# First small sums by copying and adding DMA, and one convolution tap moved to the second layer, in a two-layer kernel

## Chip, core and metric

The kernel runs on one core of a Trainium2 chip. The metric is the device time of one execution in microseconds, of three runs: 2356.79, 2358.98 and 2359.99, so a median of 2358.98 us.

## What is computed

A depthwise causal convolution over seven tokens with softmax weights for each of 8 heads, then a two-layer feed-forward with a hard-swish between, all in float32. `x` is 8 x 4096 x 192; the feed-forward is 192 to 2048 to 192 over 32768 tokens.

```python
w = softmax(weight, axis=-1)                  # 8 heads x 7 taps
out[b, s, h, g] = sum_k w[h, k] * x_pad[b, s + k, h, g]
h = out.reshape(32768, 192) @ w_in            # 192 -> 2048
g = h * np.clip(h + 3.0, 0.0, 6.0) / 6.0
y = g @ w_out                                 # 2048 -> 192
```

## The kernel before, in words

The tokens go in 32 blocks of 1024 (`TB`). The first block (block 0) is computed together with the preparation of the weights; blocks 1 to 31 run through the same two functions, `first_layer` and `second_layer`, which write out the whole order of the instructions by hand (the scheduler is in manual mode; it only adds the waits). Every engine executes its own instructions in the order in which the program gives them.

**First layer** (L499 to L562). Sixteen slots n; each computes 128 columns of the hidden layer for the 1024 tokens. A slot has 18 matmuls in three parts, HIGH, LOW and MIX (a float32 product made of three faster ones, L506). `begin(n)` issues HIGH and LOW and lets ScalarE scale the two banks (L523); for the last slot ScalarE scales the lower bank (L526) and VectorE the upper one (L527). `end(n)` issues MIX, ScalarE's relu (L302) and VectorE's gate (L306). The program runs `begin` two slots ahead of `end`. Slots 0 to 7 read the block's own tokens (`y_own`), slots 8 to 15 read the same tokens with the partition halves swapped (`y_other`, swapped by DMA, L265 to L267). Slots 0 to 7 fill the quarters A11 and A22 of the hidden activations `g`, slots 8 to 15 A21 and A12. Each quarter is 128 partitions by 8 chunks by 512 tokens. Between the slots stand jobs: `jobs` holds the convolution taps of the next block (L1033, one VectorE instruction each), and after them come small sums for the second layer.

**Second layer** (L604 to L891). The product with `w_out` is done by a Strassen-like scheme (Winograd's form, seven products): S1 = A21 + A22, S2 = S1 - A11, S3 = A11 - A21, S4 = A12 - S2, and the products n = 1 to 7 of `prod` (L417). S1, S2 and S4 are formed in place over A21, A11 and S3. S1 is formed by adding DMAs (`third_sum`, L564): GpSimd issues a transfer with `accum_op=add` of a pair of chunks, 512 KB, once the same pair of S3 has been taken from A21. Products 1, 2, 4 and 5 are cut once more in the same way for a part of the output (`small`, L657): their small sums s1 to s4 of the four parts of a quarter (`small_sums`, L575) lie in `shared` (of A11), `sums4[0]` (of A22), `sums2` (of A12) and `s5` (of S1, over A22). The fourth small sum of A22 and of A12 (`last_sum`, L703) and S4 (`negative`, L700) are formed by `difference` (L696): ScalarE writes the negative of one operand, then a DMA issued by GpSimd adds the other.

TensorE works here in four columns of 32 (streams 0 to 3). `put` gives each matmul a place on a clock of 80 units, one unit being 256 tokens; `do(t, fn)` puts other engines' work between the matmuls at t - 0.5. L885 sorts all of it by clock, and so fixes the order in which each engine gets its instructions. `plain(j, bank, n, q, chunks)` puts product n's matmuls over chunks into stream j, `level_two` (L727) puts the small products in an order and, behind each, a copy on ScalarE that hands the partial sum to the next accumulator (`steps`). `fill` puts pieces of product 5 into gaps of stream 3.

`between` (L1099 to L1107) holds the work for later blocks: splitting the next block's `y` into HIGH, LOW and MIX (L1050 to L1060), swapping them, loading x of the block after (`begin_conv`, on SP's queue) and that block's first convolution product on ScalarE (L1031). The tile `x` has one buffer, so a load waits for the last tap that reads it. `shared` also holds the outputs of the block before, which are stored from there.

Stores and x loads are issued by SP, the swaps and all adding DMAs by GpSimd. All run on the core's 16 DMA engines.

Of the kernel before, what the change touches and what calls it, by code (L numbers as in the profile page):

```python
# [8 lines left out]
ALU = mybir.AluOpType  # L9
# [16 lines left out]
def kernel(  # L26
# [472 lines left out]
    def first_layer(i, jobs):  # L499
# [44 lines left out]
        for n in range(count):  # L544
            if n == count - 3:
                begin(n + 2)
            end(n)
            if n < count - 3:
                begin(n + 2)
            for job in jobs.get(n, ()):  # L550
                job()
            if n < NP and n % 2:
                small_sums(shared, A11, (1, 2, 3, 4), nc.gpsimd, every[n - 1 : n + 1])
            if n == NP:
                sums4[:] = [pools[0].tile([P, NP, N], F32, name="z4", tag="own")]
                small_sums(sums4[0], A22, (1,), nc.gpsimd)
            if n == count - 3:
                small_sums(sums4[0], A22, (2,), nc.vector)
            if n in (NP + 1, NP + 3, NP + 5):
                third_sum((n - NP - 1) // 2, nc.gpsimd if n < NP + 5 else nc.vector)  # L560
            if n == NP + 1:
                small_sums(sums4[0], A22, (3,), nc.gpsimd)  # L562

    def third_sum(p, engine):  # L564
        pair = slice(2 * p, 2 * p + 2)
        g_sums(engine, (3,), range(NP)[pair], 2)
        nc.gpsimd.dma_start(out=S1[:, pair], in_=A22[:, pair], accum_op=ALU.add)  # L567
# [7 lines left out]
    def small_sums(to, x, which, engine=nc.gpsimd, r=every):  # L575

        r = slice(r[0], r[-1] + 1)
        x11, x12, x21, x22 = four_parts(x[:, r])
        s1, s2, s3, s4 = four_parts(to[:, r])
        forms = {  # L580
            1: (s1, x21, x22, ALU.add), 2: (s2, s1, x11, ALU.subtract),
            3: (s3, x11, x21, ALU.subtract), 4: (s4, x12, s2, ALU.subtract),
        }
        for n in which:
            o, p, q, op = forms[n]
            engine.tensor_tensor(out=o, in0=p, in1=q, op=op)  # L586
# [17 lines left out]
    def second_layer(i, between):  # L604
# [91 lines left out]
        def difference(out, x, y):  # L696
            nc.scalar.mul(out, y, -1.0)  # L697
            nc.gpsimd.dma_start(out=out, in_=x, accum_op=ALU.add)  # L698

# [47 lines left out]
        def fill(k):  # L747
            plain(3, b, 5, 2, [chunks.pop(0) for _ in range(k)], first_fill.pop() if first_fill else False)
# [41 lines left out]
        level_two(5, lambda: late["p5"], (1,))  # L790
        plain(3, a, 2, 2, every[2:6])
        last or fill(2)
# [21 lines left out]
        do(0, small_sums, sums2, A12, (1, 2), nc.vector)  # L814
        do(5, last_sum, sums4[0], A22)
        do(6, third_sum, 3, nc.vector)
        do(7, small_sums, sums2, A12, (3,), nc.vector)
# [3 lines left out]
        do(33, g_sums, nc.vector, (2,), every[4:], 4)  # L821
# [3 lines left out]
        do(36, small_sums, s5, S1, (1, 2, 3, 4), nc.vector)  # L825
# [87 lines left out]
    with tc.manual_schedule():  # L913
# [144 lines left out]
        def split_mix():  # L1058
            high, low, mix = y_own
            from_high(mix[:], high[:], 1.0 + EPS, y[:], ALU.subtract)  # L1060
# [30 lines left out]
        for i in range(1, NB):  # L1091
            jobs = {n: [tap] for n, tap in zip((-1, 1, 3, 5, 8, 11), taps)}
# [7 lines left out]
            if i + 1 < NB:  # L1100
                between += [(37, split_high), (56, split_low), (63, split_mix)]
                between += [
                    (t, lambda n=n: swap_parts(nc.gpsimd, (n,)))
                    for n, t in ((HIGH, 70), (LOW, 70), (MIX, 70))
                ]
            if i + 2 < NB:
                between += [(1, begin_conv), (74, lambda: conv[0]())]  # L1107
            left = second_layer(i, between)
            taps = conv[1:]
# [33 lines left out]
```

## Time and profile before

| What | Value |
|---|---|
| runs | 2356.79, 2358.98, 2359.99 us |
| the profiled execution: time, span | 2358.78, 2357.0 us |
| mean granted TensorE clock | 0.997 |
| blocks 1 to 31 start at | 99.75 us; block 31 at 2273.8 us |
| a middle block (13), from 969.45 us | 72.45 us: first layer 35.34, second 37.11 |
| first layer's matmuls in a block | 288, 128x512, 0.113 us apart |
| second layer's | 80 units of 0.43 us |
| ScalarE's scaling L523, relu L302 | 1.01, 1.11 us |
| VectorE's gate L306, tap L1033 | 1.21, 2.25 us (mean) |
| adding DMAs, per block | 4 of g, 4 of s, 2 of z, 512 KB each |
| DMA traffic | 296.94 MB, 126 GB/s in the mean |

The profile is one execution, taken by the hardware profiler. Its page gives for each engine its busy time, the share of the span and the number of instructions, then the groups of instructions by line and shape, with how long the engine idled before them and what released it. PE is TensorE's matmuls, PEld its weight loads, DVE is VectorE, ACT ScalarE, POOL GpSimd, SP SyncE. L636 is line 636 of the kernel. Names such as `z<-g` are the tile written and the tile read: `z` is the tile of the small sums of A22 and of A12, `s` is S3, `shared` the small sums of A11 and the outputs. A float32 matmul of the second layer stands in the trace as two instructions. The waits list says who waited for whom, the total, how many times and the longest; the timeline gives start, duration, engine, line, operation, and in brackets the idle time before it with what ended it.

### The profile page before, as it was taken

To read this page: it belongs to the slowest core of one execution; us is meant where nothing else is said; L and a number is where in the kernel's file an instruction comes from. 1 tells how busy PE (TensorE), PEld (TensorE's weight loads), DVE (VectorE), ACT (ScalarE), POOL (GpSimd) and SP (SyncE) were. 2 spreads that over 40 slices of the span, in tenths; PEclk is the share of its full clock that TensorE was granted. 3 is DMA by queue.
4 is the path that set the end of the run, shared out by engine and by line. 5 is a ranking of instruction groups with operands and counts; after the bars stand their busy time and mean duration, and the time that the engine had idled before them with its cause. 6 is when DMAs were issued, how large, how long until landed. Compare 5 with 4: busy or idle time off the path is not lost.

```text
span 2357.0 us, 55204 instructions
## 1 busy us (share of the span) xinstructions
PE 2276.9 (97%) x22984; PEld 1508.2 (64%) x22984; DVE 2027.7 (86%) x1859; ACT 1762.2 (75%) x2391; POOL 1338.0 (57%) x1157
## 2 busy tenths in 40 slices
PE   9999999999999999999999999999999999999998
PEld 5456666566666566666676656666666766666664
DVE  8888988888888898888888888888889888888876
ACT  7578787777777787777878777777778777777875
POOL 2456664466654666545666446665466654566644
PEclk9999999999999999999999999999999999999999
DMA  5376668866678666687666886667866668766576
GB/s 148 68 128 120 123 112 148 145 116 122 117 132 157 112 122 123 116 157 132 119 123 114 144 150 113 120 119 129 157 115 123 123 113 158 135 118 123 107 135 104
DMA packets 336939, 296.94 MB, mean 126 GB/s; under 512 B 211984, under 2 KB 248848, under 8 KB 336688
## 3 DMA queue, kind: packets, MB, share of 16 engines
q0 software_dynamic: 114976, 234.46, 55.8%
q1 hardware_dynamic: 220472, 58.67, 13.9%
q8 instruction: 181, 2.97, 0.5%
q14 instruction: 70, 0.57, 0.1%
q10 hardware_dynamic: 1240, 0.27, 0.1%
HBM read 31.72 MB, written 25.17 MB: 24 GB/s over the span
## 4 chain that ended last, share of the span: by engine, by line
PE 55%; ACT 12%; DMA 12%; DVE 11%; issue 9%; POOL 1%; DVEq 0%; SPq 0%; ACTq 0%; POOLq 0%
PE psum L636 30%; PE psum L511 22%; DMA z<-g 11%; ACT g L302 6%; DVE g L306 5%; ACT psum L523 3%; DVE y L1033 3%; PE psum L296 2%; PE psum L341 2%; ACT psum L633 1%; DVE s L414 1%; DVE psum L527 1%; POOL g L567 1%; ACT z L735 0%; ACT shared L735 0%
## 5 line engine op out<-in xcount | busy, mean ns | idle before, releaser
L636 PE MATMUL psum<-g,w_out 128*32 128x512 f32 (+1 forms) x5968 | 893.4, 506 | 3.9 <-DMA g<-g 3.9
L636 PE MATMUL psum<-s,w_out 128*32 128x512 f32 (+1 forms) x3024 | 692.3, 587 | 1.5 <-DMA s<-g 1.5
L306 DVE SCALAR_TENSOR_TENSOR g<-g,psum 128x1024 f32<-128x1024 f32 (+1 forms) x528 | 613.0, 1181 | 75.6 <-ACT g L302 75.2
L302 ACT ACTIVATE g<-psum,half 128x1024 f32<-128x1024 f32 (+1 forms) x528 | 568.1, 1087 | 38.1 <-PE psum L511 37.3
L511 PE MATMUL psum<-y_other,w_in 64*128 64x512 f32 x4464 | 542.4, 391 | 42.8 <-DVE psum L527 41.4
L511 PE MATMUL psum<-y_own,w_in 64*128 64x512 f32 x4464 | 523.8, 390 | 0.0
L511 PEld LDWEIGHTS psum<-y_other,w_in 64*128 64x128 f32 x4464 | 418.4, 184 | 156.1 <-DVE psum L527 53.6
L523 ACT ACTIVATE psum<-psum 128x1024 f32<-128x1024 f32 x465 | 468.7, 1008 | 62.1 <-PE psum L511 56.6
L636 PEld LDWEIGHTS psum<-g,w_out 128*32 128x32 f32 x5968 | 361.3, 110 | 219.5 <-issue 105.1
L586 POOL TENSOR_TENSOR shared<-g 128x256 f32<-128x256 f32 x248 | 365.3, 1473 | 237.6 <-DVE g L306 237.6
L511 PEld LDWEIGHTS psum<-y_own,w_in 64*128 64x128 f32 x4464 | 422.6, 184 | 108.9 <-issue 26.0
L1033 DVE SCALAR_TENSOR_TENSOR y<-x,c_sb,y 128x1536 f32<-128x1536 f32 x186 | 418.6, 2251 | 1.5 <-ACT y L1031 1.3
L698 POOL DMA_DIRECT2D s<-g x124 | 148.4, 1197 | 266.6 <-ACT s L697 266.6
L636 PE MATMUL psum<-g,w_s 128*32 128x256 f32 x1488 | 283.0, 380 | 0.0
L636 PE MATMUL psum<-z,w_out 128*32 128x256 f32 x992 | 235.9, 381 | 23.7 <-DMA z<-g 21.2
L636 PE MATMUL psum<-z,w_s 128*32 128x256 f32 x992 | 236.7, 382 | 0.2 <-DVE z L586 0.2
L567 POOL DMA_DIRECT2D g<-g x124 | 149.5, 1206 | 152.5 <-DVE s L414 130.3
L636 PEld LDWEIGHTS psum<-s,w_out 128*32 128x32 f32 x3024 | 181.9, 110 | 70.7 <-issue 32.9
L636 PEld LDWEIGHTS psum<-z,w_out 128*32 128x32 f32 x992 | 103.7, 110 | 125.3 <-DMA z<-g 47.6
L266 POOL DMA_DIRECT2D y_other<-y_own x90 | 47.9, 532 | 236.0 <-DVE shared L458 235.9
L414 DVE TENSOR_TENSOR g<-g 128x2048 f32<-128x2048 f32 x62 | 142.1, 2293 | 32.8 <-issue 31.7
L586 POOL TENSOR_TENSOR z<-g 128x1024 f32<-128x1024 f32 x62 | 163.2, 2632 | 0.0
(114 smaller groups left out, 2932.8 us busy)
## 6 DMA issues: line engine op xcount, KB each, us to landing
y_other<-y_own POOLq DMA_DIRECT2D x180, 384.0 KB, 8.0
g<-g POOLq DMA_DIRECT2D x124, 512.0 KB, 6.5
s<-g POOLq DMA_DIRECT2D x124, 512.0 KB, 6.4
z<-g POOLq DMA_DIRECT2D x62, 512.0 KB, 8.3
out_dram<-shared SPq DMA_DIRECT2D x378, 64.0 KB, 4.3
x<-in_x_dram SPq DMA_DIRECT2D x53, 388.5 KB, 7.7
stage<-in_moe_w_in_dram SPq DMA_DIRECT2D x16, 192.0 KB, 4.4
stage<-in_moe_w_out_dram SPq DMA_DIRECT2D x8, 384.0 KB, 5.6
```

Of the source, the lines that this page charges most:

```text
L266: dma.dma_start(out=to[D2:P], in_=part[0:D2])
L296: nc.tensor.matmul(out=psum[:, b], lhsT=w[r], rhs=src, start=start, stop=stop, skip_group_check=onto,)
L302: nc.scalar.activation(r6, h, ACT.Relu, bias=half[:], scale=1.0 / 6.0)
L306: nc.vector.scalar_tensor_tensor(out=g_, in0=g_, scalar=1.0, in1=h, op0=ALU.min, op1=ALU.mult)
L414: engine.tensor_tensor(out=o[:, r], in0=a[:, r], in1=b[:, r], op=op)
L511: nc.tensor.matmul(out=psum[:, 2 * slots[n] + k], lhsT=r32(w_in_parts[part][r, c, s]), rhs=r32(y_other[0][r, part, s] if group else y_own[ ...
L523: nc.scalar.mul(both(n), both(n), 4097.0)
L567: nc.gpsimd.dma_start(out=S1[:, pair], in_=A22[:, pair], accum_op=ALU.add)
L586: engine.tensor_tensor(out=o, in0=p, in1=q, op=op)
L636: nc.tensor.matmul(out=out, lhsT=w, rhs=x, start=start, stop=True, tile_position=(0, j * QS), skip_group_check=True,)
L698: nc.gpsimd.dma_start(out=out, in_=x, accum_op=ALU.add)
L1033: jobs.append(lambda k=k: nc.vector.scalar_tensor_tensor(out=y[:], in0=x[:, :, k : k + N], scalar=c_sb[:, k : k + 1], in1=y[:], op0=ALU.mu ...
```

## The change

In the first layer the sum s1 = x21 + x22 of A11 and of A22 is no longer computed by GpSimd. Once slots 0 to 7 are done, SP issues for each a DMA that copies x21 to s1, and one slot later GpSimd issues for each a DMA that adds x22. The second small sum, until now s1 - x11, is written as x22 - s3, which is the same since s3 = x11 - x21, so that it follows the third. The third sum of A22 is formed by `difference` at slot 8: ScalarE writes -x21, an adding DMA adds x11. A22's second sum moves from VectorE at slot 13 to GpSimd at slot 11.

S3's pairs 0 and 1 stay on GpSimd at slots 9 and 11; pair 2 moves from VectorE at slot 13 to VectorE at the second layer's start; pair 3 is formed by `difference` (ScalarE and an adding DMA) in place of VectorE. The adding DMAs of S1's pairs 2 and 3 are issued in the second layer behind A22's fourth sum and S3's last pair.

In the second layer the first small product of product 5 moves from clock 36 to 44 (not in the last block), and four plain matmuls of product 2 move ahead of it. The small sums of S1 on VectorE are done third and second first, ahead of the second half of S2, then first and fourth. The second convolution product of the block after next (a tap on VectorE) moves from the first layer into the second, at 62, and the first one on ScalarE from 74 to 58. MIX is computed from LOW and HIGH in place of `y` and HIGH, at 70; the swaps stand at 69, 69 and 71.

```diff
--- before.py
+++ after.py
@@ -550,21 +550,37 @@
             for job in jobs.get(n, ()):
                 job()
             if n < NP and n % 2:
-                small_sums(shared, A11, (1, 2, 3, 4), nc.gpsimd, every[n - 1 : n + 1])
+                small_sums(shared, A11, (3, 2, 4), nc.gpsimd, every[n - 1 : n + 1])
             if n == NP:
                 sums4[:] = [pools[0].tile([P, NP, N], F32, name="z4", tag="own")]
-                small_sums(sums4[0], A22, (1,), nc.gpsimd)
-            if n == count - 3:
-                small_sums(sums4[0], A22, (2,), nc.vector)
-            if n in (NP + 1, NP + 3, NP + 5):
-                third_sum((n - NP - 1) // 2, nc.gpsimd if n < NP + 5 else nc.vector)
+                for to, x in ((shared, A11), (sums4[0], A22)):
+                    nc.sync.dma_start(out=four_parts(to)[0], in_=four_parts(x)[2])
+                difference(four_parts(sums4[0])[2], four_parts(A22)[0], four_parts(A22)[2])
             if n == NP + 1:
-                small_sums(sums4[0], A22, (3,), nc.gpsimd)
-
-    def third_sum(p, engine):
-        pair = slice(2 * p, 2 * p + 2)
-        g_sums(engine, (3,), range(NP)[pair], 2)
-        nc.gpsimd.dma_start(out=S1[:, pair], in_=A22[:, pair], accum_op=ALU.add)
+                third_sum(0)
+                add_pair(0)
+                for to, x in ((shared, A11), (sums4[0], A22)):
+                    adding(four_parts(to)[0], four_parts(x)[3])
+            if n == NP + 3:
+                small_sums(sums4[0], A22, (2,), nc.gpsimd)
+                third_sum(1)
+                add_pair(1)
+
+    def adding(out, x):
+        nc.gpsimd.dma_start(out=out, in_=x, accum_op=ALU.add)
+
+    def difference(out, x, y):
+        nc.scalar.mul(out, y, -1.0)
+        adding(out, x)
+
+    def pair_of(p):
+        return slice(2 * p, 2 * p + 2)
+
+    def third_sum(p, engine=nc.gpsimd):
+        g_sums(engine, (3,), every[pair_of(p)], 2)
+
+    def add_pair(p):
+        adding(S1[:, pair_of(p)], A22[:, pair_of(p)])
 
     TH = N // 2
     halves = slice(0, TH), slice(TH, N)
@@ -578,7 +594,7 @@
         x11, x12, x21, x22 = four_parts(x[:, r])
         s1, s2, s3, s4 = four_parts(to[:, r])
         forms = {
-            1: (s1, x21, x22, ALU.add), 2: (s2, s1, x11, ALU.subtract),
+            1: (s1, x21, x22, ALU.add), 2: (s2, x22, s3, ALU.subtract),
             3: (s3, x11, x21, ALU.subtract), 4: (s4, x12, s2, ALU.subtract),
         }
         for n in which:
@@ -693,10 +709,6 @@
             add(p[second, hi], p[second, hi], p[second, lo])
             add(p[second, lo], m136, p[second, lo])
 
-        def difference(out, x, y):
-            nc.scalar.mul(out, y, -1.0)
-            nc.gpsimd.dma_start(out=out, in_=x, accum_op=ALU.add)
-
         def negative(pair):
             difference(S3[:, pair], A12[:, pair], S2[:, pair])
 
@@ -787,9 +799,11 @@
         fill_half(0, 4) if last else fill(2)
         level_two(1, lambda: p1, rest)
         fill_half(0, 4) if last else fill(2)
-        level_two(5, lambda: late["p5"], (1,))
+        last and level_two(5, lambda: late["p5"], (1,))
         plain(3, a, 2, 2, every[2:6])
-        last or fill(2)
+        if not last:
+            level_two(5, lambda: late["p5"], (1,))
+            fill(2)
         level_two(5, lambda: late["p5"], rest)
         fill_half(1, 8) if last else fill(2)
         assert clock == [80] * 4
@@ -811,18 +825,21 @@
         def fold_with(p, j=3):
             fold(p, chains[j][2])
 
-        do(0, small_sums, sums2, A12, (1, 2), nc.vector)
-        do(5, last_sum, sums4[0], A22)
-        do(6, third_sum, 3, nc.vector)
-        do(7, small_sums, sums2, A12, (3,), nc.vector)
+        do(4.5, last_sum, sums4[0], A22)
+        do(1, third_sum, 2, nc.vector)
+        do(6, lambda: difference(S3[:, pair_of(3)], A11[:, pair_of(3)], A21[:, pair_of(3)]))
+        do(6, add_pair, 2)
+        do(6, add_pair, 3)
+        do(7, small_sums, sums2, A12, (3, 2, 1), nc.vector)
         do(28.5, g_sums, nc.vector, (2,), every[:4], 4)
         do(32, tiles)
         do(32, fold_with, p1)
-        do(33, g_sums, nc.vector, (2,), every[4:], 4)
+        do(35, small_sums, s5, S1, (3, 2), nc.vector)
+        do(35.5, g_sums, nc.vector, (2,), every[4:], 4)
         do(32.5, fold_with, p4, 2)
         do(36, copy, out=b[m], in_=p1)
         do(21, last_sum, sums2, A12)
-        do(36, small_sums, s5, S1, (1, 2, 3, 4), nc.vector)
+        do(36, small_sums, s5, S1, (1, 4), nc.vector)
         for n, t in zip(range(0, NP, 2), (34, 39, 42, 45)):
             do(t, negative, slice(n, n + 2))
         do(45.5, lambda: copy(out=late["p7"], in_=c[m]))
@@ -1057,7 +1074,7 @@
 
         def split_mix():
             high, low, mix = y_own
-            from_high(mix[:], high[:], 1.0 + EPS, y[:], ALU.subtract)
+            from_high(mix[:], high[:], EPS, low[:], ALU.subtract)
 
         def prepare():
             for n in range(0, NP, 4):
@@ -1089,7 +1106,7 @@
         left = []
         taps = conv[2:]
         for i in range(1, NB):
-            jobs = {n: [tap] for n, tap in zip((-1, 1, 3, 5, 8, 11), taps)}
+            jobs = {n: [tap] for n, tap in zip((-1, 1, 3, 5, 8), taps)}
             jobs[-1] = left + jobs.get(-1, [])
             first_layer(i, jobs)
             def begin_conv():
@@ -1098,15 +1115,15 @@
 
             between, conv = [], []
             if i + 1 < NB:
-                between += [(37, split_high), (56, split_low), (63, split_mix)]
+                between += [(37, split_high), (57, split_low), (70, split_mix)]
                 between += [
                     (t, lambda n=n: swap_parts(nc.gpsimd, (n,)))
-                    for n, t in ((HIGH, 70), (LOW, 70), (MIX, 70))
+                    for n, t in ((HIGH, 69), (LOW, 69), (MIX, 71))
                 ]
             if i + 2 < NB:
-                between += [(1, begin_conv), (74, lambda: conv[0]())]
+                between += [(1, begin_conv), (58, lambda: conv[0]()), (62, lambda: conv[1]())]
             left = second_layer(i, between)
-            taps = conv[1:]
+            taps = conv[2:]
 
 
 # ---- launch: one core; inputs and outputs as the reference has them ----
```

## Prediction

> **What bounds the kernel now.** I read first the page's busy times, then the whole list of waits, then one middle block (969.45 to 1041.90 us, 72.45 us long) in stretches, then its queues in order of time.
>
> ```profile
> PE 2276.9 (97%) x22984; PEld 1508.2 (64%) x22984; DVE 2027.7 (86%) x1859; ACT 1762.2 (75%) x2391; POOL 1338.0 (57%) x1157
> ```
>
> The waits give the total in us, how many, and the longest:
>
> ```profile
> PE psum L511 <- DVE psum L527: 41.4, 29, 1.5
> PE psum L636 <- DMA z<-g: 21.2, 29, 1.4
> ```
>
> TensorE is the bound, and it stands still in two places of each block: at the end of the first layer, where the last scaling waits on VectorE, and in the second layer, where the fourth sum of A22 has not landed. Per block that is 1.4 and 0.7 us by PE's rows; matmul starts, which show the pace, lose about 1.7 us at each.
>
> The first place, VectorE in order of time:
>
> ```profile
> 998.71 3.38 DVE L1033 SCALAR_TENSOR_TENSOR y<-x,c_sb,y 128x1536 f32<-128x1536 f32 x1
> 1002.02 1.21 DVE L306 SCALAR_TENSOR_TENSOR g<-g,psum 128x1024 f32<-128x1024 f32 x1
> 1003.15 0.69 DVE L527 TENSOR_SCALAR psum<-psum 128x512 f32<-128x512 f32 x1
> ```
>
> The convolution tap of slot 11 took 3.38 us (1.78 where GpSimd is quiet), and the scaling L527 stands behind it.
>
> The second place needs the DMA engines. The stretches below have PE, PEld, DVE, ACT, POOL busy, then PEclk, the DMA engines' share, GB/s:
>
> ```profile
> 969.45:982.45 13.00, 13.00 (x117) 10.99 (x116) 11.36 (x11) 11.49 (x12) 5.20 (x7) 1.00 0.99 207
> 982.45:992.45 10.00, 9.96 (x88) 7.83 (x86) 9.69 (x8) 9.52 (x11) 9.77 (x11) 1.00 0.01 2
> 992.45:1001.45 9.00, 9.00 (x84) 7.44 (x82) 8.18 (x5) 8.60 (x9) 8.70 (x6) 1.00 0.01 2
> 1005.95:1009.45 3.50, 3.50 (x44) 2.08 (x40) 3.50 (x3) 1.81 (x4) 2.18 (x3) 1.00 1.04 236
> 1009.45:1024.45 15.00, 14.21 (x181) 8.45 (x177) 11.74 (x12) 9.20 (x21) 5.17 (x5) 1.00 1.09 176
> 1024.45:1038.45 14.00, 14.00 (x174) 7.48 (x170) 11.96 (x14) 10.26 (x17) 4.38 (x4) 1.00 0.96 161
> ```
>
> The DMA engines idle for 19 us of the first layer and are full through the second. GpSimd issues the adding DMAs one after another:
>
> ```profile
> 1009.27 1.20 POOL L567 DMA_DIRECT2D g<-g  x1 [1.01 <-DVE s L414]
> 1010.93 1.28 POOL L698 DMA_DIRECT2D z<-g  x1 [0.46 <-ACT psum L732]
> 1015.20 1.18 POOL L567 DMA_DIRECT2D g<-g  x1 [2.98 <-DVE s L414]
> 1016.94 1.28 POOL L698 DMA_DIRECT2D z<-g  x1 [0.57 <-PE psum L636]
> ```
>
> By the trace's landings these four and the pair before them (issued at 1007.04) landed at 43.5, 46.1, 49.6, 52.2 and 55.1 us from the block's start: in order, 2.6 us apart for a pair sum (2 KB packets) and 3.5 and 2.9 us for a fourth sum (1 KB packets). So a full queue serves a pair in 2.6 and a strided sum in 3.2 us. The S3 negations behind them landed 3.1, 3.1 and 3.3 us apart.
>
> **The change, part by part.** Times are from the block's start.
>
> *Tap and sums off VectorE in the first layer.* The slot 11 tap (3.38), A22's second sum (2.96 beside GpSimd) and the third pair's S3 (1.21) leave VectorE before the end of the layer. Against this ScalarE gets one multiplication at slot 8 (1.06, as L697) in a queue without slack: L523 and L302 start 0.92 and 1.12 us apart, 2.04 per slot, and PE's 18 matmuls at 0.113 take 2.04. The lag stays to the end of the layer, but each scaling is needed only 1.03 us after it ends, and 0.35 us of idle is there at slot 10. I charge 0.3. The last block's first layer, without the wait, took 33.0 us, the typical one 35.34; I take 33.3, bounds 33.0 and 34.4. In itself this is worth 2.0 us.
>
> *GpSimd* loses four ops of 0.74 and two 128x1024 sums (2.4 each) and gains one such sum and four issues of 1.2. It is not the bound; it only sets when DMAs start.
>
> *Six more transfers of 512 KB per block*: two copies on SP's queue, two adds onto them, A22's third, S3's last pair. The trace has no plain 1 KB copy inside SBUF. Bounds: 403 GB/s, the best slice while the x loads ran, gives 1.3 us; the slower adding row gives 3.5. I take 2.5, between the 2.2 of the x loads' mean (236 GB/s) and the 3.0 of 176 GB/s.
>
> When does this work start? The copies need the gate of slot 7, which ends at 21.3; a store's first packet comes 1.4 us after its issue, so 22.7. The x tile is free after the tap of slot 8 (24.5) and no longer after that of slot 11 (32.6), so both x loads (3.4 us, the 1005.95 stretch) move up into the same stretch. GpSimd's issues: A22's third at 25.4 (behind its sums of A11 and the multiplication), pair 0 at 29.0, the two adds at 30.7 and 32.4, then A22's second sum and S3's second pair (2.4 each), pair 1 at 38.3, the fourth sum at 39.9, S3's last pair at 41.6, pairs 2 and 3 at 43.2 and 44.9 (spaced 1.66, as 1009.27 to 1010.93). Each starts moving 1.8 us after its issue (pair 0 issued at 31.33 has its first packet at 33.13), or when those ahead are done, and here those ahead are later every time. So the landing of pair 3, L, is a plain sum:
>
> 22.7 + copies 5.0 + A22's third 3.2 + x 3.4 + pair 0 2.6 + adds 6.4 + pair 1 2.6 + fourth sum 3.2 + S3's last pair 3.1 + pairs 2 and 3 5.2 + 0.3 to signal = 57.7.
>
> Before, L was 52.2.
>
> *New waits on GpSimd.* Its two adds wait for the copies (landed by 30), and A22's second sum, now x22 minus the third, waits for the third's landing: 31.2 if the x loads queue behind it, 34.6 if ahead. In the second case GpSimd stands 1.4 us, with S3's second pair, pair 1, the fourth sum and all later issues behind it; L does not move, since each of these is still issued before its turn in the line (pair 1 would be ready at 41.5, its turn is 43.3).
>
> *What hangs on pair 3.* The small sums of S1 are reordered: third and second now stand ahead of the second half of S2 on VectorE. From L: 1.14 + 1.24 for these, 2.22 for S2's half. Only then can ScalarE negate pairs 2 and 3, and the moved step of product 5 (copy of its first small product, clock 47.5 instead of 39.5) is now queued behind them: 1.06, two copies 0.73, 1.06, 0.59, the copy 0.36; with waits 8.5 us from L. The matmuls of clock 52 need that copy, and 28 units of 0.43 follow: 12.0. So a block lasts L + 20.5 = 78.2 us, 5.75 more than now. The first layer's 2.0 us are not in this sum: TensorE arrives sooner and waits longer (at units 28 and 32 for the fourth sum and S3's last pair, 49.4 and 52.5, then at 44 and 52).
>
> *The rest, at nothing.* S3's third pair (1.21) moves to the second layer's start on VectorE and S3's last pair leaves it for ScalarE (1.06, where ScalarE idles 1.6 us before L732); both are done before the transfers they feed have their turn. A12's small sums only change order; unit 24 needs them at 43.7, they end near 41. The second-layer tap (1.69) takes split_mix's old place (1.71) on VectorE; split_mix at 69.5 only delays the swap, whose last landing (10.8 us into the next block) has until the switch to the swapped parts at 19.8; without that cover each us costs one. The wait before unit 36 is for a ScalarE copy (L633) that stays. Small product (5,1) at clock 44 costs nothing by itself.
>
> **Sum.** 29 blocks at +5.75 are 167; block 30 loads no x: 5.75 - 3.4 = 2.4; in the last block the step keeps its old place, and unit 36 waits for L = 54.3 instead of running at about 51: 3.3. The profiled execution took 2358.8 us (span 2357.0, median of the runs 2359.0): 2358.8 + 172 = 2531.
>
> The ends: copies at 1.3 and each adding transfer 0.15 faster give L near 54 and +2 per block, about 2420; copies at 3.5, pairs at 2.95 (16 packets of 185 ns on each engine) and strided adds at 3.5 (32 of 110 ns) give L near 62 and +10, about 2660.
>
> **Rivals.**
>
> *Faster: the idle 19 us swallow the new traffic.* This decides when L is below 72.45 - 20.5 = 51.95. If transfers moved at 1.3 us each (403 GB/s), GpSimd's issue would set L: 44.9 + 1.8 + 1.3 + 0.3 = 48.3. Then what is left in the second layer is the chain at unit 52 even without late DMAs: from unit 32 (13.8 after the layer's start), copies and folds 2.7, sums and S2 4.6, ScalarE 3.9 end at 25.0 against 22.4, so 2.6 us; 33.3 + 34.4 + 0.4 + 2.6 = 70.7, -1.75 per block, about 2307. For it speaks the idle stretch; against it, that no adding transfer in a queue here came faster than 2.6 us. The Trainium skill's page "DMA: Bandwidth & Descriptors", section "Anatomy of one DMA — SWDGE (gpsimd) path", has this rule: about 2.0 us fixed plus bytes over 436 GB/s, so an estimated 1.2 us of moving for 512 KB. The trace disagrees for adding DMAs: 2.6 to 3.5 us, 176 GB/s. Chance 0.13; exactly even (L just at 52) 0.02.
>
> *A mild loss: what is issued in the first layer is done before the second.* Then only the last four stand in line: 41.7 + 3.2 + 3.1 + 5.2 + 0.3 = 53.5, block 74.0, +1.55 each, about 2405. It needs the two queues to move side by side at more than the 176 GB/s seen. Chance 0.12.
>
> *The first-layer wait does not go*, since ScalarE's extra 1.06 us holds the scaling back. It can be, but costs nothing while L sets the block; it is inside the forecast.
>
> **Chances.** Forecast (2420 to 2660) 0.71, mild loss 0.12, faster 0.13, even 0.02, above 2660 0.02. The range 2400 to 2660 reaches over the forecast and the mild loss. About 0.2% is what a measurement of this kernel can tell from no change. Slower 0.85, same 0.02, faster 0.13.
>
> **What would show it.** Right: the L511 wait for L527 falls under 0.3 us a block and the first layer is near 33.3; the DMA share is near 1 from about 23 us into the block to its end; pair 3 lands near 58; PE waits at the fourth sum (z), at S3's last pair, and about 5 us behind the copy of step (5,1), with ScalarE waiting for VectorE's second half of S2. Wrong: pair 3 landing before 52, adds 1.5 us apart, or no PE wait near unit 52.

## The result, and the profile after

The changed kernel took 2544.92 us (median of 4 runs, 2544.16 to 2547.92) against 2358.14 for the kernel before (2356.79 to 2359.99): ratio 1.0794, interval 1.0775 to 1.0813. The forecast was 2531, slower, so sign and size came true. The loss has the predicted place, but its size came out right by luck: two errors nearly cancel.

Below is the page's line of busy times of the changed kernel (span 2542.4 us):

```profile
PE 2349.3 (92%) x22984; PEld 1477.2 (58%) x22984; DVE 1852.9 (73%) x1797; ACT 1802.4 (71%) x2453; POOL 1296.9 (51%) x1126
```

TensorE runs the same 22984 matmuls, but is busy 92% of the span instead of 97%, and its busy time grew by 72 us: the same work went more slowly in places. Next are lines of the list of waits (total us, times, longest):

```profile
DVE g L602 <- DMA g<-g: 142.2, 30, 6.3
PE psum L652 <- ACT psum L742: 80.5, 30, 2.7
PE psum L652 <- DVE g L414: 47.7, 30, 2.8
PE psum L652 <- DMA s<-g: 35.0, 31, 1.9
PE psum L652 <- DMA z<-g: 15.1, 25, 1.4
```

The wait of L511 for VectorE's scaling is gone. In its place TensorE waits, about once per block each, for A22's fourth sum (`z`), for S3's last pair (`s`), for S2's second half (L414) and for the copy of step (5,1) (L742). The first line is the source of the waits for L414 and L742: VectorE waits for S1's pair 3. Block 13 in stretches (PE, PEld, DVE, ACT, POOL busy, PEclk, DMA share, GB/s), cut at the end of the first layer, at the landing of pair 3, and around the slow clock:

```profile
1043.07:1076.41 33.34, 33.34 (x289) 26.68 (x288) 27.58 (x24) 31.47 (x33) 21.49 (x19) 1.00 0.73 160
1076.41:1098.72 22.31, 21.46 (x259) 10.90 (x261) 12.50 (x12) 16.38 (x29) 12.91 (x10) 1.00 1.14 181
1098.72:1108.30 9.58, 5.38 (x56) 1.88 (x52) 8.59 (x6) 4.21 (x7) 3.31 (x3) 1.00 1.03 171
1108.30:1112.00 3.70, 3.70 (x31) 1.77 (x28) 0.13 (x1) 1.84 (x2) 0.10 (x1) 0.54 1.07 182
1112.00:1121.20 9.20, 9.20 (x108) 4.59 (x100) 8.44 (x12) 2.41 (x6) 3.13 (x6) 1.00 0.45 82
```

The first layer is 33.34 us (35.34 before). After pair 3 has landed TensorE stands 4.2 of 9.6 us, and right behind that stop its granted clock is 0.54 for 3.7 us. That chain, VectorE first and ScalarE below:

```profile
1098.81 2.48 DVE L602 TENSOR_TENSOR g<-g 128x1024 f32<-128x1024 f32 x2 [4.27 <-DMA g<-g]
1101.21 2.29 DVE L414 TENSOR_TENSOR g<-g 128x2048 f32<-128x2048 f32 x1
```

```profile
1103.53 1.06 ACT L573 ACTIVATE s<-g 128x1024 f32<-128x1024 f32 x1 [4.91 <-DVE g L414]
...
1105.23 1.06 ACT L573 ACTIVATE s<-g 128x1024 f32<-128x1024 f32 x1
1106.32 0.58 ACT L845 COPY shared<-psum 96x512 f32<-96x512 f32 x1
1106.92 0.34 ACT L742 COPY psum<-psum 32x256 f32<-32x256 f32 x1
```

From 1098.72 to 1107.26 this is 8.5 us, as worked out in the prediction: small sums, S2's half, two negations, and only then the copy for which unit 52 waits.

Where pair 3's landing comes from is seen in GpSimd's order of time:

```profile
1073.17 2.29 POOL L570 DMA_DIRECT2D z<-g  x1
1075.69 2.40 POOL L602 TENSOR_TENSOR z<-g,z 128x1024 f32<-128x1024 f32 x1 [0.23 <-DMA z<-g]
1078.05 2.39 POOL L414 TENSOR_TENSOR s<-g 128x1024 f32<-128x1024 f32 x1
1080.74 1.19 POOL L570 DMA_DIRECT2D g<-g  x1 [0.30 <-POOL s L414]
```

The two adds keep it until 1075.46; then come two sums, and pair 1 is issued 37.67 us into the block. Issue and landing of the transfers (us into the block, medians of blocks 2 to 29):

| Transfer | before | after |
|---|---|---|
| A22's third | none | 23.80, 32.60 |
| S1 pair 0 | 31.35, 37.42 | 28.56, 35.11 |
| adds onto s1 of A11, A22 | none | 29.33, 38.12; 30.10, 41.11 |
| S1 pair 1 | 37.62, 44.17 | 37.73, 43.80 |
| A22's fourth | 40.63, 49.61 | 38.47, 47.28 |
| S3's last pair | none | 39.26, 50.18 |
| S1 pair 2 | 39.84, 46.72 | 39.97, 52.99 |
| S1 pair 3 (L) | 45.76, 52.29 | 40.70, 55.83 |

### The profile page after: what moved, and what is told of

The parts are those of the page before. It is cut to its first block, busy times and chain, and to the rows that moved or that the text cites. A ratio compares the mean times of both kernels' runs of the same rounds, so it can differ in the third digit from the quotient of the medians.

```text
span 2542.4 us, 55545 instructions
## 1 busy us (share of the span) xinstructions
PE 2349.3 (92%) x22984; PEld 1477.2 (58%) x22984; DVE 1852.9 (73%) x1797; ACT 1802.4 (71%) x2453; POOL 1296.9 (51%) x1126
## 4 chain that ended last, share of the span: by engine, by line
PE 49%; DMA 27%; POOL 12%; issue 4%; DVE 3%; ACT 3%; SPq 0%; DVEq 0%; POOLq 0%; ACTq 0%
PE psum L511 29%; PE psum L652 18%; DMA g<-g 13%; DMA z<-g 7%; DMA s<-g 6%; POOL s L414 4%; POOL z L602 3%; POOL g L570 3%; POOL z L570 2%; DVE g L414 2%; PE psum L296 2%; PE psum L341 2%; ACT s L573 1%; DVE g L602 1%; ACT shared L845 1%
## 5 line engine op out<-in xcount | busy, mean ns | idle before, releaser
L652 PE MATMUL psum<-g,w_out 128*32 128x512 f32 (+1 forms) x5968 | 977.6, 539 | 54.9 <-DVE g L414 47.7
L652 PE MATMUL psum<-s,w_out 128*32 128x512 f32 (+1 forms) x3024 | 669.0, 587 | 35.0 <-DMA s<-g 35.0
L511 PE MATMUL psum<-y_other,w_in 64*128 64x512 f32 x4464 | 527.2, 390 | 0.0
L511 PE MATMUL psum<-y_own,w_in 64*128 64x512 f32 x4464 | 523.4, 389 | 0.0
L511 PEld LDWEIGHTS psum<-y_own,w_in 64*128 64x128 f32 x4464 | 413.5, 184 | 117.7 <-issue 26.0
L511 PEld LDWEIGHTS psum<-y_other,w_in 64*128 64x128 f32 x4464 | 413.5, 184 | 103.7 <-ACT psum L523 10.3
L570 POOL DMA_DIRECT2D s<-g x155 | 214.9, 1387 | 417.1 <-ACT s L573 369.0
L652 PE MATMUL psum<-g,w_s 128*32 128x256 f32 x1488 | 328.1, 412 | 80.5 <-ACT psum L742 80.5
L602 POOL TENSOR_TENSOR shared<-g,shared 128x256 f32<-128x256 f32 x248 | 314.0, 1266 | 89.0 <-DVE g L306 57.3
L1050 DVE SCALAR_TENSOR_TENSOR y<-x,c_sb,y 128x1536 f32<-128x1536 f32 x186 | 335.2, 1802 | 1.5 <-ACT y L1048 1.4
L573 ACT ACTIVATE s<-g 128x1024 f32<-128x1024 f32 x155 | 162.6, 1049 | 153.2 <-DVE g L414 152.5
L570 POOL DMA_DIRECT2D z<-g x124 | 205.9, 1660 | 97.1 <-PE psum L652 54.8
L602 DVE TENSOR_TENSOR g<-g 128x1024 f32<-128x1024 f32 x124 | 148.9, 1221 | 143.3 <-DMA g<-g 142.2
L652 PE MATMUL psum<-z,w_out 128*32 128x256 f32 x992 | 236.0, 381 | 15.4 <-DMA z<-g 15.1
L652 PEld LDWEIGHTS psum<-g,w_s 128*32 128x32 f32 x1488 | 132.4, 116 | 190.5 <-ACT psum L742 108.6
L414 DVE TENSOR_TENSOR g<-g 128x2048 f32<-128x2048 f32 x62 | 141.9, 2288 | 108.0 <-PE psum L652 108.0
```

The source lines that it names most:

```text
L414: engine.tensor_tensor(out=o[:, r], in0=a[:, r], in1=b[:, r], op=op)
L511: nc.tensor.matmul(out=psum[:, 2 * slots[n] + k], lhsT=r32(w_in_parts[part][r, c, s]), rhs=r32(y_other[0][r, part, s] if group else y_own[ ...
L652: nc.tensor.matmul(out=out, lhsT=w, rhs=x, start=start, stop=True, tile_position=(0, j * QS), skip_group_check=True,)
L1050: jobs.append(lambda k=k: nc.vector.scalar_tensor_tensor(out=y[:], in0=x[:, :, k : k + N], scalar=c_sb[:, k : k + 1], in1=y[:], op0=ALU.mu ...
```

## The experiments

Each ran beside the kernel before (2356.7 to 2358.4 us). "After" is the changed kernel; L is the landing of S1's pair 3.

**1. The order on ScalarE.** In after, the negations of S4's last two pairs are put behind the copy of step (5,1):

```diff
-        for n, t in zip(range(0, NP, 2), (34, 39, 42, 45)):
+        for n, t in zip(range(0, NP, 2), (34, 39, 48.4, 48.6)):
```

> The changed kernel with only ScalarE's order altered: the negations of S3's pairs 2 and 3 stand behind the copy of step (5,1). My theory: a block lasts until pair 3 of S1 lands (L, 55.8 us into the block) plus the chain that follows; with the copy ahead of the negations unit 52 waits only for the second half of S2 (4.75 us after L), so a block takes 55.8 + 4.75 + 12.05 = 72.6 instead of 78.5, and with the long stop of TensorE its half clock (PEclk 0.54 over 3.7 us behind it) goes too: 2545 - 30 x 5.9 = about 2368. If the half clock has another cause, 2 us a block stay: about 2428. Rival, the landing alone sets the block and the order costs nothing: 2545.

Measured: 2402.04 us, ratio 1.0181 (1.0160 to 1.0201), 143 us less than after. L stayed at 55.85. ScalarE in block 13, which starts at 982.19:

```profile
1039.66 0.34 ACT L742 COPY psum<-psum 32x256 f32<-32x256 f32 x1 [0.44 <-PE psum L652]
...
1042.81 2.01 ACT L573 ACTIVATE s<-g 128x1024 f32<-128x1024 f32 x2 [2.23 <-DVE g L414]
```

The copy comes 6.4 us earlier in its block (57.47 instead of 63.85) and unit 52 waits only for S2's half (1.8 us). The slow clock is gone from blocks 2 to 29 but for one stretch. So the order behind L cost most of the loss, together with the slow clock that it brought: by the mean granted clocks of the two profiles (0.974 and 0.997) I estimate the clock's part of the 143 us at up to 60. The time is 34 us above the expectation, 1.1 us per block. Of this the later negations explain about 0.2: the last one now lands at 70.95 in the median, and in 10 of blocks 2 to 29 unit 76, which needs it, stops (5.8 us in all). Stream 3 ends 0.7 us (median) behind the others (0.06 in before): in each of these blocks its copy L743 starts only when ScalarE's convolution product (L1048, 1.58 us, which the change put at 58) ends. That this is the rest was not tried.

**2. The two adds left out** (s1 of A11 and A22 then lacks x22):

```diff
                 add_pair(0)
-                for to, x in ((shared, A11), (sums4[0], A22)):
-                    adding(four_parts(to)[0], four_parts(x)[3])
```

> The changed kernel without the two adding DMAs onto the first small sums (x22 is left out of s1 of A11 and A22). Theory A, as in the prediction, one line of transfers from the copies to pair 3: L falls by the two services, 5.4 to 6.4 us, and a block with it: about 2545 - 30 x 5.4 = 2383. Theory B, formed on the profile after (block 30 loads no x, yet its L is 55.7): GpSimd issues pair 1 at 37.7, late, since its second sum of A22 waits for the third's landing, and five transfers follow, 16 us; what stood in the line before is nearly worked off by then. L falls by about 1 us at most, pair 1's issue stays near 37.5: 2515 to 2535.

Measured: 2532.96 us, ratio 1.0747 (1.0727 to 1.0766); L 55.31, only 0.5 earlier. The plain sum of the prediction, in which each transfer ahead of pair 3 counts, is refuted: two of them are gone and L hardly moves. In after the DMA engines have no pause over 0.25 us from 25.7 us to L in any of blocks 2 to 29; without the adds they stand idle for 4.8 us (median) ahead of pair 1. Below are block 13 of after from 25.70 to L, and then block 13 here (from 1038.63) from 35.7 to 39.8 (columns as above):

```profile
1068.77:1098.72 29.95, 29.10 (x323) 16.70 (x325) 16.86 (x17) 23.70 (x37) 19.87 (x14) 1.00 1.14 192
```

```profile
1074.28:1078.39 4.11, 4.11 (x53) 1.97 (x51) 4.11 (x3) 2.42 (x5) 3.81 (x4) 1.00 0.00 0
```

GpSimd's second sum still waits for A22's third (landing at 32.9 beside the x loads), and pair 1 is issued at 38.0 in block 13. Block 30 loads no x: there the third lands at 29.75, pair 1 is issued at 34.89, L is 52.13. In block 30 of after, with the adds, pair 1 is issued at 37.45 though the third has landed at 29.76, and L is 55.74. Two holds of the same length, the third's landing and the issuing of the adds, lie side by side; taking one away gains nothing. Blocks 30 and 31 (72.91 and 80.60 us, against 78.74 and 86.17) hold 11.4 of the 15.8 us between the two profiled spans (2526.6 and 2542.4).

**3. VectorE work back in the first layer** (two sums into a tile that is free there, at slot 11):

```diff
+                for _ in range(2):
+                    nc.vector.tensor_tensor(out=S3[:, 6:8], in0=A11[:, 6:8], in1=A11[:, 4:6], op=ALU.subtract)
```

> The changed kernel with two more VectorE instructions of 1.2 us at slot 11 of the first layer (a difference written to S3's last pair, which is overwritten later). It takes away most of what the moved tap gave: the scaling L527 comes later and the first layer takes about 35.0 instead of 33.3. Theory: the block is set by the landing of pair 3 and the chain behind it, so its length stays: 2545, within 10. Rival, the first layer's time counts in full: 2545 + 30 x 1.6 = 2593.

Measured: 2553.77 us, ratio 1.0824 (1.0808 to 1.0841). The first layer grew by 1.4 us (34.72), L stayed (55.86), and 1.4 x 29 = 41 us became 9. Of the 12.9 us between the profiled spans (2555.3 and 2542.4), 8.4 are in blocks 30 and 31 (84.77 and 88.56 us), and for another reason. VectorE's two added sums in block 29, then in block 30, and GpSimd's two sums there:

```profile
2332.97 2.48 DVE L566 TENSOR_TENSOR s<-g 128x1024 f32<-128x1024 f32 x2
```

```profile
2411.57 8.59 DVE L566 TENSOR_TENSOR s<-g 128x1024 f32<-128x1024 f32 x2
```

```profile
2412.89 3.88 POOL L604 TENSOR_TENSOR z<-g,z 128x1024 f32<-128x1024 f32 x1
2415.26 3.81 POOL L414 TENSOR_TENSOR s<-g 128x1024 f32<-128x1024 f32 x1
```

Blocks 30 and 31 load no x, so A22's third lands early there (29.83 in block 30, 32.78 in the median of blocks 2 to 29), GpSimd's sums meet VectorE's, all four take longer (2.4 us each is usual for GpSimd's), and TensorE stops 7.0 us for the scaling L527 (experiment 9 has the same meeting). In blocks 2 to 29 it is as the prediction has it: TensorE's early arrival is worth nothing while the block ends by L (what the clock may add to this stands in the last section).

**4. The tap alone.** The kernel before, with the second-layer tap, its splits and swaps:

```diff
-            jobs = {n: [tap] for n, tap in zip((-1, 1, 3, 5, 8, 11), taps)}
+            jobs = {n: [tap] for n, tap in zip((-1, 1, 3, 5, 8), taps)}
...
-                between += [(1, begin_conv), (74, lambda: conv[0]())]
+                between += [(1, begin_conv), (58, lambda: conv[0]()), (62, lambda: conv[1]())]
```

> The kernel before with only the tap's part of the change: five taps in the first layer, the second convolution product in the second layer, MIX from LOW, the swaps at 69, 69 and 71. The first layer falls to about 33.3 us. Theory: the landing of A22's fourth sum (49.6 us into the block) sets the rest, and it hardly moves, since pairs 1 and 2 stand ahead of it in the line: about 49.2, so TensorE waits 3 us or more at unit 28 and a block takes 71.9 to 72.3: 2340 to 2356. Rival, the first layer's gain is kept: 2359 - 29 x 2.0 = 2300.

Measured: 2355.38 us, ratio 0.9986 (0.9977 to 0.9996). The first layer fell to 33.41, and the second rose from 37.1 to about 39: S1's pair 0, issued at 31.35 as before, lands at 36.43, and the layer, which now starts 1.9 us earlier, stops for it near its start (27.1 us in 31 waits over the run, by PE's rows; 3.9 in 2 before). A22's fourth sum lands at 49.35 (49.61 before), and unit 28 stops for it (25.7 us in 22 waits; 21.2 in 29 before). The gain is given back at the next waits.

**5. S3's last pair on VectorE again**, one transfer fewer:

```diff
-        do(6, lambda: difference(S3[:, pair_of(3)], A11[:, pair_of(3)], A21[:, pair_of(3)]))
+        do(1, third_sum, 3, nc.vector)
```

> The changed kernel with S3's last pair made by VectorE in the first layer again, as pairs of the other third sums are, so that one 512-KB adding transfer (issue 41.6 in the forecast, 39.26 us in the profile of after) leaves GpSimd's queue; nothing else is changed. Queue theory: L is the issue of pair 1 plus five transfers, now four, so L comes 2.7 us earlier (55.8 to about 53.1) and each block is 2.7 us shorter, about 75.4; 29 of them are 78 us less: about 2466. If the stop at the copy of step (5,1) is still about 5 us, the half clock stays with it. Rival, L set by the fourth sum's wait and not by the number of transfers: L stays at 55.8 and the time at 2545. Rival, the extra VectorE work (1.2 us of third_sum) delays the first layer by as much: about 2500.

Measured: 2449.81 us, ratio 1.0387 (1.0374 to 1.0401); L 53.03, 2.8 earlier, as expected. That is 95 us for one 512-KB transfer behind pair 1; 2.8 us in 31 blocks are 87, and the slow clock, in 20 of blocks 2 to 29 instead of in all, may be the rest.

**6. The first small sums on GpSimd again**, without copies and adds:

```diff
-                small_sums(shared, A11, (3, 2, 4), nc.gpsimd, every[n - 1 : n + 1])
+                small_sums(shared, A11, (1, 3, 2, 4), nc.gpsimd, every[n - 1 : n + 1])
...
-                for to, x in ((shared, A11), (sums4[0], A22)):
-                    nc.sync.dma_start(out=four_parts(to)[0], in_=four_parts(x)[2])
+                small_sums(sums4[0], A22, (1,), nc.gpsimd)
...
-                for to, x in ((shared, A11), (sums4[0], A22)):
-                    adding(four_parts(to)[0], four_parts(x)[3])
```

(The first + of the second part stands behind `difference`.)

> The changed kernel with the first small sums of A11 and A22 made by GpSimd again, without the two copies and without the two adding transfers; the rest (A22's third by adding, S3's last pair by adding, the tap) stays. Theory that GpSimd's issue of pair 1 sets L: leaving the two adds out alone moved L only 0.5 us; with the copies gone and two more GpSimd sums (some 1.2 us each) ahead of its issues, pair 1 is issued at 36.5 to 38.5, so L is 54.5 to 56 and the time 2510 to 2550. Theory that the six transfers' own sum sets L: L falls by about 10 us and the time to about 2300.

Measured: 2597.34 us, ratio 1.1017 (1.1003 to 1.1032): slower than either expectation has it. GpSimd's own sums delay its issues more than the adds did: A22's third goes out at 26.73 instead of 23.80, pair 1 at 39.41, L is 57.06. So the copies and adds of the change are worth 52 us here, and a theory in which the transfers' sum sets L (2300) falls again.

**7. Experiments 1 and 5 together.**

> Two edits at once: the negations of S4's last two pairs behind the copy of step (5,1) on VectorE (as in the run that moved the negations later, 2402 us with L at 55.85), and S3's last pair on VectorE, which takes one transfer out of the queue. If the block is L plus a fixed chain, L 53.1 gives blocks 2.7 us shorter than the 73.4 of that run, about 70.7: 2402 - 31 x 2.7 = about 2320 (2300 to 2340). Rival, unit 28's wait for the fourth sum (landing 47.3, a 1.5-us stop) takes it over: blocks fall by less than 1.5, about 2360. Rival, VectorE's first layer grows by the 1.2 us of the pair: about 2350.

Measured: 2316.30 us, ratio 0.9826 (0.9813 to 0.9838), faster than the kernel before. L is 53.05; blocks 2 to 29 take 71.04 us in the mean. The two edits nearly add up (143 and 95 us from 2544.92 would be 2307): S3's last pair is worth 86 us here. (The copy is ScalarE's, not VectorE's as the expectation has it.)

**8. Experiments 1, 5 and 6 together.**

> All three undone or moved: negations behind the copy of step (5,1), S3's last pair on VectorE, first small sums of A11 and A22 on GpSimd. What is left of the change is A22's third by adding and the tap. Queue theory: pair 1 issued at about 37.5 and four transfers after it, L 52 to 53, fourth sum landing at 44 to 46 instead of 47.3, so that unit 28 no longer stops: blocks of 68.5 to 70, 2240 to 2300, faster than both kernels. Rival, the first layer grows back to 35.3 because GpSimd's sums hold VectorE's g (the wait of before): block about 71.5, about 2340. Rival, no better than before: 2358.

Measured: 2367.98 us, ratio 1.0045 (1.0032 to 1.0058): the expectation of 2240 to 2300 was wrong, and by the same 52 us that experiment 6 shows. GpSimd issues pair 0 at 33.17 (28.55 in 7), it lands at 38.22, and TensorE stops 1.7 us (mean) at unit 4, where product 5 needs it.

**9. A22's third on GpSimd** in the kernel of 7, the remaining added transfer undone:

```diff
-                difference(four_parts(sums4[0])[2], four_parts(A22)[0], four_parts(A22)[2])
+                small_sums(sums4[0], A22, (3,))
```

> The kernel of 2316 us with A22's third small sum made by GpSimd at slot 8, in place of ScalarE's negative and an adding transfer: the part of the change left in it, undone. If the wait of GpSimd's second sum for the third's landing is what holds pair 1: pair 1 is issued near 36 instead of 37.75, one transfer is gone ahead of it, the fourth sum lands near 44.7 instead of 47.3 and L near 50.3: 2260 to 2280. Rival, GpSimd's own 2.4 us for the sum cost as much as the wait (as the first small sums did: 52 us more when GpSimd made them): 2310 to 2340.

Measured: 2362.17 us, ratio 1.0017 (1.0007 to 1.0027), 46 us more than 7: wrong again, and for a reason that neither side had. VectorE and GpSimd in block 13 here, then VectorE's same tap in 7:

```profile
990.09 3.72 DVE L1050 SCALAR_TENSOR_TENSOR y<-x,c_sb,y 128x1536 f32<-128x1536 f32 x1
```

```profile
989.79 2.41 POOL L602 TENSOR_TENSOR z<-g 128x1024 f32<-128x1024 f32 x1
995.03 2.41 POOL L414 TENSOR_TENSOR s<-g 128x1024 f32<-128x1024 f32 x1 [2.83 <-DVE g L306]
```

```profile
973.83 1.81 DVE L1050 SCALAR_TENSOR_TENSOR y<-x,c_sb,y 128x1536 f32<-128x1536 f32 x1
```

The tap starts 0.3 us behind GpSimd's sum and takes 3.72 us instead of 1.81 (over 3.5 in each of blocks 2 to 29, in 7 in none): what was left of the sum, 2.1 us, and then nearly its own time. The gates behind it slip, the first layer is 34.62, and GpSimd's next sum waits 2.8 us for a gate. The Trainium skill's page "SBUF — State Buffer", section "🔬 SBUF: two separate sides", calls this an exclusive lock on a port pair: a VectorE instruction with two SBUF inputs and a GpSimd one that reads SBUF do not share, the second waits for the whole first. This trace agrees, 3.72 against 1.81.

**10. S3's last pair alone**, put into the kernel before:

```diff
-        do(6, third_sum, 3, nc.vector)
+        do(6, lambda: difference(S3[:, 6:8], A11[:, 6:8], A21[:, 6:8]))
+        do(6, lambda: nc.gpsimd.dma_start(out=S1[:, 6:8], in_=A22[:, 6:8], accum_op=ALU.add))
```

> The kernel before with one part of the change alone: S3's last pair by ScalarE's negative and an adding DMA in place of VectorE's subtraction; one transfer of 512 KB more per block, in the line ahead of pair 3. Theory that the cost is a place in the line: pair 3 lands 2.7 us later (52.3 to 55.0), but the kernel before makes S2's second half from it first and has room at unit 52 (due at 35.3 + 24.9 = 60.2, S2's half ready at 57.5): 2350 to 2375. Rival, the last negations of S4 follow 2.7 us later too and are late for products 3's units 76 and 78: up to 2400. Rival, each added transfer costs its 2.7 us whole: 2442.

Measured: 2397.11 us, ratio 1.0170 (1.0153 to 1.0186). L came 3.1 later (55.41), as expected, but units 52, 76 and 78 hardly stop. The loss is elsewhere: at unit 32, which needs S3's own pair (landing 52.60), TensorE waits 31.1 us in 31 waits over the run. It also waits at unit 16 (15.2 us in 29), whose copies stand on ScalarE behind the added multiplication (1.06, started only at 41.87, when its gate is done), but that takes the place of the wait at unit 28 (2.7 us in 7, where before has 21.2 in 29). I had looked at what the transfer delays and not at what it carries.

**11. A22's fourth on GpSimd**, behind its issue of pair 1, in the kernel of 7:

```diff
                 add_pair(1)
+                small_sums(sums4[0], A22, (4,))
...
-        do(4.5, last_sum, sums4[0], A22)
```

> The kernel of 2316 us (negations behind the copy, S3's last pair on VectorE), with A22's fourth small sum made by GpSimd behind its issue of pair 1, in place of ScalarE's negative and an adding transfer; two of the waits it has left are unit 28's for that sum's landing (1.33 us) and the chain behind L. If the DMA line is what binds: the sum (2.4 us) ends near 40 instead of landing at 47.3, pairs 2 and 3 are issued near 40.5 and 41.2 and land near 46.7 and 49.4 (before: 50.2 and 53.05), no stop at unit 28 and none in its place at unit 52 (S2's half ends near 54, due at 56.2): blocks of 69.3 to 70, 2250 to 2275. Rival, L binds and not unit 28, and does not move because the issues come later: 2305 to 2320. Rival, VectorE beside a busy GpSimd gives it back: 2316 or more.

Measured: 2282.02 us, ratio 0.9680 (0.9665 to 0.9695). L is 50.14 and unit 28's stop is gone; one at unit 24 came instead (14.6 us in 21 waits over the run, by PE's rows).

**12. The order on VectorE**, in the kernel of 11:

```diff
-        do(1, third_sum, 3, nc.vector)
...
-        do(6, add_pair, 3)
-        do(7, small_sums, sums2, A12, (3, 2, 1), nc.vector)
+        do(7, small_sums, sums2, A12, (3, 2), nc.vector)
+        do(7, third_sum, 3, nc.vector)
+        do(7, add_pair, 3)
+        do(7, small_sums, sums2, A12, (1,), nc.vector)
```

> The kernel of 2282 us with S3's last pair on VectorE behind A12's third and second small sums instead of ahead of them. Its remaining stop is 1.24 us at unit 24, which needs those sums; S3's last pair ahead of them took 3.98 us beside GpSimd's fourth sum (1.2 where GpSimd is quiet). If the order on VectorE is the cause: the sums end near 42.6, before unit 24 is due (43.7), the stop goes, pair 3 is issued near 44 and lands near 50.5 and nothing is late for it: 1.0 to 1.2 us per block, 2240 to 2255. Rival, pair 3 becomes late instead (S2's half for unit 52, due at 56.2): 2270 to 2290. Rival, the collision with GpSimd moves to A12's sums and unit 24 waits all the same: 2275 to 2285.

Measured: 2257.79 us (2256.11 to 2258.68), ratio 0.9578 (0.9565 to 0.9591), the fastest, 3 us above the expected range. Busy times, and block 13's second layer (columns as above):

```profile
PE 2233.8 (99%) x22984; PEld 1490.1 (66%) x22984; DVE 1978.1 (88%) x1828; ACT 1738.9 (77%) x2391; POOL 1291.8 (57%) x1095
```

```profile
960.46:995.94 35.48, 35.37 (x435) 19.92 (x433) 32.86 (x30) 22.73 (x42) 18.09 (x15) 1.00 1.00 165
```

TensorE is busy for 35.37 of 35.48 us; 80 units of 0.43 are 34.4. The copies and adds, A22's third by adding and the tap are all still in it.

## Why the prediction was right, and where its steps were not

*First layer 33.3:* 33.34, and worth nothing by itself (3, 4).

*The six transfers as a plain sum, L = 57.7:* L was 55.8. What was mis-sized is the start of the line. The sum has the copies move from 22.7 to 27.7 and everything else behind them. They moved from 20.84 to 24.05 (block 13), 1.6 us each, near the cheap bound of 1.3, and then the DMA engines stood idle until A22's third, issued at 23.80, began to move at 25.70. So the copies are not in L at all, and the line starts 2.0 us earlier than in the sum. From there to L the sum has 30.0 us, and it took 30.1. GpSimd's issues, put 1.66 us apart, came 0.72 to 0.78 apart; that changed nothing, since the line was full.

The wrong step is to take this line for the only bound. That "each of these is still issued before its turn in the line" held in after, but with no room: pair 1, issued at 37.73, could move at about 39.6 (1.9 us later, as A22's third), when the adds were nearly done (the second landed at 41.11). GpSimd's order is thus a second bound, only 0.5 us below the first, and experiment 2 shows it: with the adds gone the line waits for GpSimd's issue of pair 1. With five transfers from pair 1 on, L came 17.2 to 18.3 us behind that issue (after, 2, both their blocks 30, and 6), with four 15.1 to 15.3 (5, 7, 8, 9). In these runs a transfer counts if it stands behind that issue, as S3's last pair does, or delays it.

*From L to the end of the block, 20.5:* the chain to the copy was 8.5 us, as worked out; the rest was 13.9 instead of 12.0 in block 13 (1107.32 to 1121.20). The granted clock was not in the sum, and 3.7 us at 0.54 lose 1.7. Product 3's 16 units, the last of the block, run without a stop in blocks 2 to 29, so the last negation holds nothing. L 1.9 too late and this 1.9 too short made 78.2 against 78.13 in block 13, and 78.51 in the mean of blocks 2 to 29: that is luck.

*Block 30 at only +2.4:* wrong, it took 78.74 (72.12 before, +6.6). Without x loads the third lands earlier, but the line then stands idle for 1.0 us until pair 0, issued at 28.56, begins to move, and the issuing of the adds still holds GpSimd (2). *The last block at +3.3:* 86.17 against 83.19, +3.0.

*The waits:* all came where they were put: by PE's rows (medians) 0.6 us at unit 28, 1.2 at 32, and 1.6 and 2.7 at 52. Matmul starts lose about 5 us at unit 52, as the prediction has it.

*Rivals:* L was above 51.95, so the idle 19 us did not swallow all of the traffic. L lies between the mild loss (53.5) and the forecast (57.7), and the mild loss had part of the mechanism: what is issued early was nearly done when pair 1 could move.

What the parts cost is measured by taking each away: the negations ahead of the copy 143 us with what the slow clock adds (1), S3's last pair by DMA 95 (5), the copies and adds a gain of 52 (6), A22's third a gain of 46 (9, in the kernel of 7), the tap a gain of 3 in the kernel before (4). They need not add up.

## What to carry to other kernels

Before pricing an added transfer, ask behind which issue the landing that ends the stage hangs: transfers ahead of it in an idle stretch may be free, one behind it costs its whole service time, and the consumer of its own data may be the next one late. Look at the in-order queues behind that landing: a changed order on ScalarE cost more here than any transfer (143 us against 95, the slow clock included in both). A sum moved to GpSimd is not free either, since it delays GpSimd's issues and holds up VectorE.

## What the hardware showed that I had not expected

**The clock.** In after, the granted clock fell to 0.5 once in each of blocks 1 to 30, for 3.41 us in most and 6.83 in the others, in or behind the 5-us stop; all these stretches start at one phase of a 3.413-us grid, to 0.01 us. With the stop shortened to under 2 us (1) they vanish from all but one of these blocks, so the stop causes them; with one of 2.9 us (5) they came in 20 of blocks 2 to 29. (Before has a single one in these blocks too, in block 27.) Blocks 2 to 29 took 78.51 us in the mean, 23.00 times 3.413; with the adds left out 22.96 times, with VectorE's extra work 23.04, with S3's last pair on VectorE 22.06; without the stop 21.57 and 20.81 (1, 7), where no whole number is to be seen. It looks as if the grid pinned the blocks, which would also have swallowed part of the small effects in 2 and 3. That is argued from these numbers and was not tried by itself; experiment 6 (23.55, its blocks alternating) shows that it need not settle. The Trainium skill's page "TensorE: Matmul & The Clock Gate", section "🔬 Part 1: The HAM clock gate (the "warmup" mystery)", states a free-running window of 3413 ns and a half clock after an idle one; the trace agrees with the grid to 0.01 us, and adds that a stop of 5 us with six matmuls in its middle is enough, and in 20 of 28 blocks of experiment 5 one of 2.9 us, which is shorter than the window.

**Transfers and issues.** Plain 1 KB copies inside SBUF, two of 512 KB on SP's queue, took 45 to 52 ns a packet (5th to 95th percentile) and 3.2 us together, some 330 GB/s, where adding packets of 1 KB took 101 to 127 ns. GpSimd's issues, 1.66 us apart in the rows of before that the prediction reads, came 0.72 to 0.78 us apart in after when nothing held them; in before, too, A22's fourth sum follows pair 2 by 0.79 in the median.
